# First convolution stage as pairs of 64-row TensorE tiles: an S5 scan gated with an H3 long convolution

## The chip, the cores and the metric

The kernel runs on one core of one Trainium2 chip. The metric is device time in microseconds (us). All kernels of one comparison were run in turns with the kernel before on the same chip. A run is called slow when it lies over 1.5% above the fastest run of the same kernel, otherwise fast; averages and ratios here use fast runs. On one core the times of one kernel spread by up to 18 us, so differences below 1% are not read as differences.

## The reference

`S = 2048`, `D = 1024`, batch 1, bfloat16. `A` is a diagonal complex scan, `B` a long convolution by FFT, and a scalar gate for each row mixes them. Cut to what matters:

```python
def _B_ref(q, k, v, shift_k, ssm_k, ssm_D):          # q is A's x
    k_shift = ...                                    # causal filter of 4 taps per channel
    kv = k_shift * v
    y = irfft(rfft(pad(kv)) * rfft(pad(ssm_k)))[:S]  # causal convolution, length 2 S
    y = y + kv * ssm_D[None, None, :]                # the skip weight: one number per channel
    return q * y

g = sigmoid((x * gate_w).sum(-1, keepdims=True))
return g * _A_ref(...) + (1 - g) * _B_ref(x, ...)
```

## The kernel before

The transform of B is three products on TensorE. The channels come in 8 units of 128; of each unit the filter (K) and the input (V) are transformed. TensorE writes its products to PSUM, where this kernel has four tiles of 1024 columns; an evacuation copies such a tile to SBUF, from which the next step reads. A tile of K or V holds 8 channels x 16 time blocks on its 128 partitions, and `NG = 16` groups of 8 channels along the free dimension. The skip weight of a channel is added to sample 0 of its filter, so the tile `sdz` must hold the 8 channels of each group at partitions 0, 16, 32, ... 112.

```python
sdz = parm.tile([128, D // 8], BF16, name="sdz")
nc.vector.memset(sdz, 0.0)
...
dma("POOL", 0.6, lambda: [sdz[0:128:16, :]], lambda: [B_ssm_D.rearrange("(g c) -> c g", c=8)], [], [e_sdz], -200, issue=1.3)
...
def load_A(src, u, tag, ex, pr):                       # K and V tiles of unit u
    t = pl.tile(tag, [NG, 128], cap=CAPS[tag])
    ...
    dma("SP", 2.6, lambda: [t.ap],
        lambda: [src[u * CH:(u + 1) * CH, :].rearrange("(g c) (n m) -> (c n) g m", c=8, m=128)], ...)
    return t

def load_K(u, pr):
    ka = load_A(B_ssm_k, u, "ka", [], pr)
    op("POOL", 0.25, lambda: G.tensor_tensor(out=ka.ap[:, :, 0], in0=ka.ap[:, :, 0],
                                             in1=sdz[:, u * NG:(u + 1) * NG], op=ALU.add), ...)     # line 712
    return ka

def stage1(a, z, w, hh, q, pr):                        # first stage: half of the frequencies, 8 groups
    ps = pl.psum([8, 128])
    def f():
        for i in range(8):
            PE_.matmul(ps.ap[:, i, :], lhsT=a.ap[:, 8 * q + i, :],
                       rhs=t1v[:, hh * 128:(hh + 1) * 128], start=True, stop=True)                   # line 747
    ...
    evac(...)                                          # 1024 columns of PSUM to SBUF: line 520

def spec(z, kv, q, h, pr):                             # second stage: K and V in one product
    ...                                                # 512 + 256 + 256 columns: lines 760 to 762
...
for hh in range(2):
    z = pl.tile("z", [8, 2, 2, CH], cap=CAPS["z"])
    for w, a in ((0, ka), (1, va)):
        for q in range(2):
            stage1(a, z, w, hh, q, PU[u][4 + hh])
    ...
```

`op`, `dma` and `evac` only record work. A list scheduler in the kernel then puts all of it into one fixed order for each engine, from tables of priorities (`PS`, `PU`, ...) and limits on buffers (`CAPS`). Each engine runs its list in that order.

Of the kernel before, what the change touches and what calls it, by code (L numbers as in the profile page):

```python
# [317 lines left out]
def kernel(  # L318
# [35 lines left out]
    CH = 128  # L354
# [24 lines left out]
    sdz = parm.tile([128, D // 8], BF16, name="sdz")  # L379
# [116 lines left out]
    tab1 = tabB.tile([128, 16, 2, 8], BF16, name="tab1")  # L496
# [22 lines left out]
    def evac(o_, i_, r, w, prio):  # L519
# [14 lines left out]
        [-427.2, -1083.5, 24.9, -780.9, -204.2, -1089.3, -324.2, -515.8, 71.9, -210.3, -1260.0],  # L534
        [-705.1, -403.6, -901.1, -494.7, -729.5, -287.3, 776.9, -570.5, -705.6, -264.3, -450.7],
        [-241.3, -302.5, -542.0, -230.8, 110.9, -574.5, 18.1, 98.8, 142.7, -769.2, -1187.5],
        [-225.3, 90.4, 3.4, -430.0, -212.3, -234.6, 58.5, -724.3, -681.9, -757.6, -1901.0],
        [-528.6, -87.6, -252.8, 51.9, 179.0, -229.1, -57.5, 217.6, 119.4, -179.2, -15.2],
        [221.2, 154.3, -430.1, -56.0, 24.2, 36.2, -482.5, -303.7, 42.6, -546.0, -514.0],
        [-484.3, -185.5, 228.0, -404.7, 149.7, -608.8, -117.9, -305.2, -587.6, -145.3, 214.0],  # L540
        [-81.2, 181.0, -870.6, -304.1, 273.2, -35.7, 66.5, 89.8, 407.7, 271.4, -321.5],
    ]
    PU = [
        [-862.5, -1665.1, -1164.4, -497.9, -793.6, -334.9, -898.2, -892.9, -899.2, 53.0, -342.8, -919.3, -1021.7, -1138.5],
        [-1197.2, -576.0, -1859.3, -750.4, -783.4, 108.2, -1211.7, -134.4, -1391.3, -625.7, -695.6, 142.7, -637.3, -830.0],
        [-883.6, -901.4, -2192.4, -135.2, -397.8, -167.7, -1038.5, -632.4, -741.0, -663.6, -443.3, -348.2, -828.9, -1858.3],
        [-422.2, -1524.9, -3002.1, -1789.7, -1628.2, 76.7, -624.4, -596.7, -1807.9, -986.0, 184.4, -868.7, -1101.3, -453.1],
        [-1177.7, -1058.3, -1227.0, -197.3, -955.1, 51.0, -1415.8, -423.8, -625.9, -1309.6, -1493.1, -858.4, -368.7, -1156.3],
        [160.1, -1665.5, -1080.4, -319.6, -1177.1, 24.7, -1055.3, -275.2, -281.5, -3.8, -843.5, -1118.8, -63.9, -235.7],
        [231.4, -1719.5, -1931.1, -946.9, -964.7, -516.2, -2023.7, -1096.3, -1171.2, -731.8, -165.3, -925.9, -519.7, -974.1],  # L550
        [-2013.4, -1902.6, -1933.6, -1026.0, -1145.7, -1011.7, -2629.3, -759.8, -1134.2, -798.7, -1034.3, -1752.8, -590.0, -664.0],
    ]
    PO = [
        [377.3, 600.4, -823.5],
        [377.4, 168.1, -139.0],
        [-920.1, 1298.4, -120.6],
        [151.9, 1173.6, -754.1],
        [-377.5, 767.6, -407.2],
        [-390.4, 1063.7, -1054.5],
        [-355.6, 9.3, -1223.6],  # L560
        [-280.7, 495.1, -101.3],
        [189.0, 211.4, 204.3],
        [326.3, 111.7, -677.7],
        [-344.9, 809.2, -296.6],
        [-174.6, 1110.7, -1287.9],
        [-133.8, -647.5, -506.5],
        [-72.6, 147.9, 591.6],
        [58.1, 1181.8, -738.2],
        [-520.2, 1310.1, -136.3],
    ]  # L570
    PC = [
        [88.8, 259.5],
        [91.2, 5.4],
        [216.3, -500.6],
        [296.5, 69.5],
        [-522.8, 410.3],
        [-241.8, -85.2],
        [-663.7, 231.4],
        [-168.9, -283.4],
    ]  # L580
    PH = [-489.3, 277.9, -35.3, -417.3, -0.7, -305.5, -324.5, -501.8]
    PG = [-435.2, -508.5, -1259.5, -564.5, -677.8, 588.3]
    PX = [95.0, 1.8]
    CAPS = {"zb": 9, "Hc": 10, "tab": 7, "z": 10, "kv": 6, "qq": 9, "ra": 3, "rb": 12, "kT": 1, "vT": 2, "acc": 1, "ka": 1, "va": 1, "pp": 1,
            "tmpj": 2, "t1": 2, "xn": 3, "xt": 4, "pb": 5, "ot": 10, "BT": 2, "xs": 3, "dg": 7, "cw": 4, "tgZ": 8, "frt": 5, "rqt": 10, "Hk": 12}
    SPARE, NBIG, NKEEP, NPX = 0, 4, 4, 1
# [3 lines left out]
    dma("POOL", 0.6, lambda: [sdz[0:128:16, :]], lambda: [B_ssm_D.rearrange("(g c) -> c g", c=8)], [], [e_sdz], -200, issue=1.3)  # L590
# [27 lines left out]
    def tables0():  # L618
# [12 lines left out]
        v2c, v2s = sl(88, 16), sl(104, 16)  # L631
        v1 = pl.tile("tg4", [16, 2], F32, cap=1)
# [25 lines left out]
        def c():  # L658
            TT(out=tab1.rearrange("p k r c -> p (k r) c"),
               in0=v1.ap.rearrange("p k r -> p (k r)").unsqueeze(2).to_broadcast([128, 32, 8]),  # L660
               in1=mask().unsqueeze(1).to_broadcast([128, 32, 8]), op=ALU.mult)
            for vt, tt in ((v2c, tabFc), (v2s, tabFs)):
                TT(out=tt, in0=vt().unsqueeze(2).to_broadcast([128, 16, 8]),
                   in1=masks().unsqueeze(1).to_broadcast([128, 16, 8]), op=ALU.mult)
# [36 lines left out]
    def conv():  # L701
        def load_A(src, u, tag, ex, pr):
            t = pl.tile(tag, [NG, 128], cap=CAPS[tag])
            ex = ex + ([(xT[0, NC - 1], 1)] if u < 2 else [])
            dma("SP", 2.6, lambda: [t.ap],
                lambda: [src[u * CH:(u + 1) * CH, :].rearrange("(g c) (n m) -> (c n) g m", c=8, m=128)],
                ex, [t], pr, alt="POOL", alt_issue=1.8)
            return t

        def load_K(u, pr):  # L710
            ka = load_A(B_ssm_k, u, "ka", [], pr)
            op("POOL", 0.25, lambda: G.tensor_tensor(out=ka.ap[:, :, 0], in0=ka.ap[:, :, 0], in1=sdz[:, u * NG:(u + 1) * NG], op=ALU.add),  # L712
               r=[ka, e_sdz], w=[ka], prio=pr)
            return ka
# [27 lines left out]
        def stage1(a, z, w, hh, q, pr):  # L742
            ps = pl.psum([8, 128])

            def f():
                for i in range(8):
                    PE_.matmul(ps.ap[:, i, :], lhsT=a.ap[:, 8 * q + i, :], rhs=t1v[:, hh * 128:(hh + 1) * 128],  # L747
                               start=True, stop=True)
            op("PE", 8 * 0.058, f, r=[a, e_t1, (e_g, 0), (e_g, 1)], w=[ps], prio=pr)
            evac(lambda: z.ap[:, :, w, :, 64 * q:64 * q + 64].rearrange("p k r (g c) -> p k r g c", c=8), lambda: ps.ap.rearrange("p g (k r c) -> p k r g c", r=2, c=8),  # L750
               r=[ps], w=[(z, (w, q))], prio=pr)

        def spec(z, kv, q, h, pr):
            ps = pl.psum([2, 2, 2, CH])

            def f():
                for i in range(2):
                    k2 = 4 * q + 2 * h + i
                    zz = z.ap[:, k2 % 8]
                    PE_.matmul(ps.ap[:, i], lhsT=fC[:, k2, :], rhs=zz, start=True, stop=False)  # L760
                    PE_.matmul(ps.ap[:, i, :, 0, :], lhsT=fS[:, k2, :], rhs=zz[:, :, 1, :], start=False, stop=False)  # L761
                    PE_.matmul(ps.ap[:, i, :, 1, :], lhsT=fN[:, k2, :], rhs=zz[:, :, 0, :], start=False, stop=True)  # L762
            op("PE", 2 * (MM(512) + 2 * MM(256)), f, r=[z, e_f], w=[ps], prio=pr)
            evac(lambda: kv.ap[:, :, :, 2 * h:2 * h + 2, :].rearrange("p w r k c -> p k (w r) c"), lambda: ps.ap.rearrange("p k w r c -> p k (w r) c"), r=[ps], w=[(kv, h)], prio=pr)
# [49 lines left out]
        for u in range(NU):  # L814
# [5 lines left out]
            for hh in range(2):  # L820
                z = pl.tile("z", [8, 2, 2, CH], cap=CAPS["z"])
                for w, a in ((0, ka), (1, va)):
                    for q in range(2):
                        stage1(a, z, w, hh, q, PU[u][4 + hh])
                for q in (2 * hh, 2 * hh + 1):
                    pr = PU[u][6 + q]
                    kv = pl.tile("kv", [2, 2, 4, CH], cap=CAPS["kv"])
                    spec(z, kv, q, 0, pr)
                    spec(z, kv, q, 1, pr + 1.0)
                    pp = product(kv, pr + 2.0)  # L830
                    inverse(pp, zb, q, pr + 3.0)
# [4 lines left out]
    def s5():  # L836
# [159 lines left out]
        wps = pl.psum([2, 512])  # L996

        def keep():
            i2 = ident.unsqueeze(1).to_broadcast([128, 2, 128])
            for _ in range(16):  # L1000
                for j in range(2):
                    PE_.matmul(wps.ap[64 * j:64 * j + 64, 0, 0:128], lhsT=ident[:, 64 * j:64 * j + 64], rhs=ident, start=True, stop=True)
            for _ in range(6):
                for j in range(2):
                    PE_.matmul(wps.ap[64 * j:64 * j + 64, 0, 0:256].rearrange("p (a b) -> p a b", b=128), lhsT=ident[:, 64 * j:64 * j + 64],
                               rhs=i2, start=True, stop=True)
            for _ in range(5):
# [183 lines left out]
```

## Time and profile before

| | before |
|---|---|
| time, median (3 runs) | 435.83 us (435.67 to 2371.7; the last figure is one stray run) |
| profiled run | 428.82 us, span 427.0, fast |
| TensorE busy | 398.4 us, 93% of the span |
| VectorE, ScalarE, GpSimd busy | 346.7, 267.8, 132.7 us |

In the page's picture of the span in 40 slices of 10.7 us, each digit is a busy share in tenths; PEclk is the clock that TensorE was granted. From the third slice on TensorE is nearly full, at full clock.

```profile
PE   7598999999999789999969999899989999999996
PEclk9999999999999999999998999999999999999999
```

The costliest groups are given as: engine and operation, count | busy us, mean ns of one | idle before them. Evacuating 1024 columns takes 1.04 us, and a first-stage product of eight matmuls is one such evacuation.

```profile
L520 ACT CAST slab<-ps 128x1024 bf16<-128x1024 f32 x197 | 185.4, 1042 | 62.8 <-PE ps L892 17.6
...
L747 PE MATMUL ps<-tab,slab 128*128 128x128 bf16 x512 | 35.0, 222 | 7.5 <-POOL slab L712 6.2
```

The list of DMA issues gives size of one transfer and median time from issue to landing: the 2 KB of skip weights take longer than the 8 KB of short-filter taps on the same queue.

```profile
skb<-in_B_shift_k_dram POOLq DMA_DIRECT2D x1, 8.0 KB, 6.3
sdz<-in_B_ssm_D_dram POOLq DMA_DIRECT2D x1, 2.0 KB, 10.2
```

### The profile page before, as it was taken

To read this page: it belongs to the slowest core of one execution; us is meant where nothing else is said; L and a number is where in the kernel's file an instruction comes from. 1 tells how busy PE (TensorE), PEld (TensorE's weight loads), DVE (VectorE), ACT (ScalarE), POOL (GpSimd) and SP (SyncE) were. 2 spreads that over 40 slices of the span, in tenths; PEclk is the share of its full clock that TensorE was granted. 3 is DMA by queue.
4 is the path that set the end of the run, shared out by engine and by line. 5 is a ranking of instruction groups with operands and counts; after the bars stand their busy time and mean duration, and the time that the engine had idled before them with its cause. 6 is when DMAs were issued, how large, how long until landed. Compare 5 with 4: busy or idle time off the path is not lost.

```text
span 427.0 us, 7194 instructions
## 1 busy us (share of the span) xinstructions
PE 398.4 (93%) x2691; PEld 228.5 (54%) x2736; DVE 346.7 (81%) x513; ACT 267.8 (63%) x310; POOL 132.7 (31%) x172
## 2 busy tenths in 40 slices
PE   7598999999999789999969999899989999999996
PEld 6353544655566456566635655676544444444442
DVE  4998999999979789989889989979696969724422
ACT  3489488747589679477966786999554286203100
POOL 6994611232464134753634403340010000000000
PEclk9999999999999999999998999999999999999999
DMA  8999999459999999598999369999989996405111
GB/s 149 113 196 195 194 232 231 174 90 160 158 186 193 256 217 185 127 207 173 187 184 164 90 192 166 287 184 178 174 163 185 213 234 205 143 22 177 49 37 62
DMA packets 153596, 71.87 MB, mean 168 GB/s; under 512 B 129861, under 2 KB 147541, under 8 KB 153561
## 3 DMA queue, kind: packets, MB, share of 16 engines
q1 hardware_dynamic: 146120, 54.55, 69.8%
q0 software_dynamic: 7360, 16.85, 16.9%
q8 instruction: 21, 0.34, 0.4%
q14 instruction: 15, 0.11, 0.1%
q10 hardware_dynamic: 80, 0.01, 0.0%
HBM read 24.93 MB, written 16.79 MB: 98 GB/s over the span
## 4 chain that ended last, share of the span: by engine, by line
PE 68%; DMA 11%; SPq 10%; ACT 4%; DVE 3%; issue 3%; POOL 0%; DVEq 0%; ACTq 0%; POOLq 0%
PE ps L1125 22%; PE ps L882 20%; SPq L513 8%; DMA slab<-slab 5%; PE ps L760 4%; ACT slab L520 4%; PE ps L747 4%; DMA slab<-in_A_x_dram 4%; PE ps L889 3%; PE ps L950 3%; DMA slab<-in_B_ssm_k_dram 3%; PE ps L761 2%; PE ps L786 2%; PE ps L762 2%; SPq L515 2%
## 5 line engine op out<-in xcount | busy, mean ns | idle before, releaser
L520 ACT CAST slab<-ps 128x1024 bf16<-128x1024 f32 x197 | 185.4, 1042 | 62.8 <-PE ps L892 17.6
L882 PE MATMUL ps<-slab,slab 128*128 128x512 bf16 (+1 forms) x527 | 115.8, 370 | 6.3 <-DMA slab<-in_A_B_re_dram 3.1
L1125 PE MATMUL ps<-slab,slab 128*128 128x512 bf16 x485 | 109.1, 379 | 1.0 <-DVE slab L1134 0.4
L882 PEld LDWEIGHTS <-slab 128*128 128x128 bf16 x544 | 52.8, 99 | 60.0 <-issue 5.5
L1125 PEld LDWEIGHTS <-slab 128*128 128x128 bf16 x512 | 49.8, 98 | 59.6 <-issue 0.7
L515 POOL DMA_DIRECT2D slab<-slab x84 | 51.4, 618 | 57.8 <-ACT slab L520 51.9
L1134 DVE SCALAR_TENSOR_TENSOR slab<-ps,gcols,slab 128x512 bf16<-128x512 f32 x32 | 23.6, 747 | 39.1 <-PE ps L1125 36.1
L1107 ACT ACTIVATE slab<-slab,omgc 128x512 bf16<-128x512 bf16 x32 | 21.2, 714 | 45.2 <-DMA slab<-pB_scr 40.1
L760 PE MATMUL ps<-slab,fC 128*128 128x512 bf16 x118 | 44.9, 381 | 1.1 <-ACT slab L520 0.6
L747 PE MATMUL ps<-tab,slab 128*128 128x128 bf16 x512 | 35.0, 222 | 7.5 <-POOL slab L712 6.2
L911 DVE TENSOR_TENSOR slab<-slab,slab 128x2048 bf16<-128x2048 bf16 x31 | 37.7, 1217 | 3.5 <-PE ps L747 1.5
L772 DVE TENSOR_TENSOR slab<-slab 128x2048 bf16<-128x2048 bf16 x32 | 38.6, 1215 | 1.8 <-ACT slab L520 1.5
L747 PEld LDWEIGHTS <-slab 128*128 128x128 bf16 x512 | 31.4, 99 | 12.3 <-POOL slab L712 6.8
L761 PE MATMUL ps<-slab,fS 128*128 128x256 bf16 x128 | 35.0, 273 | 0.6 <-issue 0.2
L762 PE MATMUL ps<-slab,fN 128*128 128x256 bf16 x128 | 35.0, 274 | 0.0
L786 PE MATMUL ps<-slab,gC 128*128 128x256 bf16 x128 | 29.9, 273 | 1.7 <-DVE slab L776 1.7
L776 DVE TENSOR_TENSOR slab<-slab 128x512 bf16<-128x512 bf16 x64 | 24.9, 416 | 6.3 <-PE ps L950 2.3
L788 PE MATMUL ps<-slab,gS 128*128 128x128 bf16 x128 | 28.0, 219 | 0.0
L787 PE MATMUL ps<-slab,gN 128*128 128x128 bf16 x128 | 28.0, 219 | 0.0
L735 DVE TENSOR_TENSOR slab<-slab,slab 128x2047 bf16<-128x2047 bf16 (+2 forms) x22 | 26.7, 1213 | 0.0
L808 DVE TENSOR_TENSOR slab<-ps,slab 128x1024 bf16<-128x1024 f32 x16 | 19.3, 1216 | 3.3 <-PE ps L806 2.8
L1113 DVE SCALAR_TENSOR_TENSOR slab<-slab,gcols,slab 128x512 bf16<-128x512 bf16 x26 | 18.3, 745 | 3.5 <-ACT slab L1107 3.4
(184 smaller groups left out, 532.5 us busy)
## 6 DMA issues: line engine op xcount, KB each, us to landing
slab<-in_A_x_dram SPq DMA_DIRECT2D x22, 256.0 KB
slab<-slab POOLq DMA_DIRECT2D x84, 64.0 KB, 5.3
slab<-h_scr SPq DMA_DIRECT2D x8, 512.0 KB
slab<-pB_scr SPq DMA_DIRECT2D x16, 256.0 KB
out_dram<-slab SPq DMA_DIRECT2D x15, 256.0 KB
slab<-in_B_ssm_k_dram SPq DMA_DIRECT2D x7, 512.0 KB
pB_scr<-slab SPq DMA_DIRECT2D x12, 256.0 KB
slab<-slab SPq DMA_DIRECT2D x44, 64.0 KB
```

The source lines that it names most:

```text
L513: nc.sync.dma_start_transpose(out=o_, in_=i_)
L515: QS[q].dma_start(out=o_, in_=i_)
L520: op("ACT", 1.04, lambda: A.copy(o_(), i_()), r=r, w=w, prio=prio, alt=("DVE", 1.2, lambda: V.tensor_copy(o_(), i_())))
L747: PE_.matmul(ps.ap[:, i, :], lhsT=a.ap[:, 8 * q + i, :], rhs=t1v[:, hh * 128:(hh + 1) * 128], start=True, stop=True)
L760: PE_.matmul(ps.ap[:, i], lhsT=fC[:, k2, :], rhs=zz, start=True, stop=False)
L761: PE_.matmul(ps.ap[:, i, :, 0, :], lhsT=fS[:, k2, :], rhs=zz[:, :, 1, :], start=False, stop=False)
L762: PE_.matmul(ps.ap[:, i, :, 1, :], lhsT=fN[:, k2, :], rhs=zz[:, :, 0, :], start=False, stop=True)
L772: TT(out=T.ap, in0=K.unsqueeze(2).to_broadcast([128, 2, 2, 4 * CH]), in1=W_.unsqueeze(1).to_broadcast([128, 2, 2, 4 * CH]), op=ALU.mult)
L786: PE_.matmul(ps.ap[:, i], lhsT=gC[:, k2, :], rhs=pp.ap[:, :, i, :], start=True, stop=False)
L882: PE_.matmul(ps.ap[:, ri, k0:k1], lhsT=BT.ap[:, d, ri, :], rhs=t.ap[:, d, k0:k1], start=(d == 0), stop=(par == 1 and d == ND - 1))
L911: TT(out=out, in0=tab.ap.unsqueeze(2).to_broadcast([128, 2, 2, CW]), in1=x.unsqueeze(1).to_broadcast([128, 2, 2, CW]), op=ALU.mult)
L1125: PE_.matmul(ps.ap, lhsT=Hr[pi, a // 4].ap[:, par, ri, (a % 4) * 128:(a % 4 + 1) * 128], rhs=CT[pi, dh][0].ap[:, CT[pi, dh][1], ri, :], st ...
```

## The change

The first stage multiplies by a block-diagonal table: 8 channels share the 128 rows, so most of the table is zero. The change gives four channels to each half of the rows and runs the halves as two 64-row tiles of TensorE side by side. A table for four channels is half as wide, so all 16 frequencies fit into 128 columns, and a unit needs half the steps. Around it, K and V get separate tiles `z`, each loaded tile comes as two halves of four-channel groups, the skip weights must stand at four partitions of each half, the warm-up is simplified, and the plan is made anew. The core of the diff, with the tables cut:

```diff
-    sdz = parm.tile([128, D // 8], BF16, name="sdz")
+    sdz = parm.tile([128, D // 4], BF16, name="sdz")
...
-    tab1 = tabB.tile([128, 16, 2, 8], BF16, name="tab1")
+    tab1 = tabB.tile([128, 16, 2, 4], BF16, name="tab1")
... (tables PS, PU, PO, PC, PH, PG, PX and CAPS all replaced; SPARE, NBIG = 0, 4 becomes 3, 3)
-    dma("POOL", 0.6, lambda: [sdz[0:128:16, :]], lambda: [B_ssm_D.rearrange("(g c) -> c g", c=8)], [], [e_sdz], -200, issue=1.3)
+    dma("POOL", 0.6, lambda: [sdz[64 * i:64 * i + 64:16, :] for i in range(2)],
+        lambda: [B_ssm_D.rearrange("(g c) -> c g", c=4)] * 2, [], [e_sdz], -200, n=2, issue=0.9)
...  load_A
-            dma("SP", 2.6, lambda: [t.ap],
-                lambda: [src[u * CH:(u + 1) * CH, :].rearrange("(g c) (n m) -> (c n) g m", c=8, m=128)],
+            dma("SP", 2.6, lambda: [t.ap[64 * i:64 * i + 64] for i in range(2)],
+                lambda: [src[u * CH + 64 * i:u * CH + 64 * i + 64, :].rearrange("(g c) (n m) -> (c n) g m", c=4, m=128) for i in range(2)],
...  load_K: one addition on GpSimd becomes two
...  stage1
-                for i in range(8):
-                    PE_.matmul(ps.ap[:, i, :], lhsT=a.ap[:, 8 * q + i, :], rhs=t1v[:, hh * 128:(hh + 1) * 128],
-                               start=True, stop=True)
+                for g in range(4):
+                    for i in range(2):
+                        rows = slice(64 * i, 64 * i + 64)
+                        PE_.matmul(ps.ap[:, 4 * i + g, :], lhsT=a.ap[rows, 4 * q + g, :], rhs=t1v[rows, :], start=True, stop=True)
...  spec: one product over K and V (512 + 256 + 256 columns) becomes one for each (256 + 128 + 128)
-            for hh in range(2):
-                z = pl.tile("z", [8, 2, 2, CH], cap=CAPS["z"])
-                for w, a in ((0, ka), (1, va)):
-                    for q in range(2):
-                        stage1(a, z, w, hh, q, PU[u][4 + hh])
+            for w, a in ((0, ka), (1, va)):
+                zs.append(pl.tile("z", [16, 2, CH], cap=CAPS["z"]))
+                for q in range(4):
+                    stage1(a, zs[w], q, PU[u][4 + w])
```

## The prediction

> **What bounds the kernel now.** I read the page first for busy shares, then the chain that ended last for what sets the end, then the costliest groups, the waits, and short timeline windows for the cost of single matmuls.
>
> ```profile
> span 427.0 us, 7194 instructions
> PE 398.4 (93%) x2691; PEld 228.5 (54%) x2736; DVE 346.7 (81%) x513; ACT 267.8 (63%) x310; POOL 132.7 (31%) x172
> ...
> PE 68%; DMA 11%; SPq 10%; ACT 4%; DVE 3%; issue 3%; POOL 0%; DVEq 0%; ACTq 0%; POOLq 0%
> ```
>
> TensorE is busy 93% of the span and carries 68% of the chain, so its time counts. Busy time overstates a matmul, because their recorded durations overlap. So I take the step from one start to the next. The chain of the last 120 us gives it for 512 columns, and one piece of the same chain gives it for the first conv stage (line 747):
>
> ```profile
> 80.31 0.27 PE ps L760
> ...
> 95.29 0.89 PE ps L747 x16
> ...
> 353.05 10.74 PE ps L1125 x49
> ```
>
> 10.74 / 49 = 0.219 us per 512-column matmul including the ends (the median step, taken from the starts in the trace, is 0.216), and 0.89 / 16 = 0.056 us per 128-column one. The 256-column step is 0.109 us, the difference of the two starts here:
>
> ```profile
> 80.42 0.27 PE L761 MATMUL ps<-slab,fS 128*128 128x256 bf16 x1
> 80.53 0.27 PE L762 MATMUL ps<-slab,fN 128*128 128x256 bf16 x1
> ```
>
> Multiplying each group by its median step, with some slack for short waits, I get 384 us of TensorE work; of the 421 us between its first and its last matmul some 37 to 42 are idle. About 13 of these lie before 36 us, where the transposed loads of x and B set the pace. The largest later idle times are three of 3.6, 1.8 and 2.9 us at 147, 218 and 222 us. After 311 us, only the output product runs (512 x 0.216 = 110.6 us in all).
>
> VectorE is the next engine: in the stretch from 25 to 300 us it is busy 252 of 275 us, as full as TensorE. ScalarE has room.
>
> **What the Trainium skill says.** (1) "TensorE: Matmul & The Clock Gate", Back-to-back issue gap: a warm matmul takes N/2.4 + 2.5 ns. That is 56, 109 and 216 ns at 128, 256 and 512 columns, and the trace agrees. (2) The same page, Part 3 on packing small matmuls: row tiles at different rows run at the same time, starting about 4 ns apart. (3) "TensorEngine Tiling (Array Packing)", Key Properties: changing the tiling mode drains the engine. The kernel before happens to contain a test of both in its warm-up:
>
> ```profile
> 8.44 0.75 PE L1010 MATMUL ps<-ident 64*64 64x128 bf16 x20
> 9.12 0.50 PE L1014 MATMUL ps<-ident 64*128 64x256 bf16 x6
> 9.55 0.62 PE L604 MATMUL ps<-dskd,ones 128*128 128x128 bf16 x8
> ...
> 37.22 1.69 PE L964 MATMUL ps<-slab,gwb 128*32 128x512 bf16 x27
> 38.84 0.39 PE L882 MATMUL ps<-slab,slab 128*128 128x512 bf16 x1
> ```
>
> Line 1014 is three pairs of 64-row tiles. One such matmul lasts 0.269 us, so the last one starts at 9.12 + 0.50 - 0.27 = 9.35: six matmuls of 256 columns start within 0.23 us, two pair-steps of about 0.115. In single file they would need 5 x 0.109 = 0.55. So pairs do run at once. The drain shows too: the last pair has streamed in by 9.35 + 0.11 = 9.46, but line 604 in full mode starts at 9.55, **about 0.09 us lost**. Leaving the 32-column tiles of the gates (lines 964 to 882) costs the same: the last starts at 38.53, has streamed by 38.74, and 38.84 is the next start. (4) The page on tiling, Gotcha 1: different row tiles must write to different PSUM banks. The new code does so (pair member i writes slots 4i to 4i+3, one bank each).
>
> **The change, part by part.**
> First stage: 512 matmuls of 128 rows and 128 columns become 512 of 64 rows and 128 columns, two at a time. Before: 512 x 0.056 = 28.7 us. After: 256 pairs x 0.056 = 14.3. **Saves 14.3 us.** The evacuations stay 64 of 1024 columns; ScalarE's copies last 0.99 to 1.17 us over very different patterns, so runs of 4 instead of 8 elements should not matter.
> Second stage (lines 760 to 762): each product over K and V together (512 + 256 + 256 columns) becomes one for each. 384 matmuls (128 x 0.216 + 256 x 0.109 = 55.6 us) become 768 (256 x 0.109 + 512 x 0.056 = 56.6). **Adds 1.0 us.** The inverse (lines 786 to 788) already has this 256 + 128 + 128 shape and steps by 0.109 + 0.056 + 0.056, so the doubled weight loads stay hidden.
> Mode switches: each unbroken run of first-stage matmuls now costs a drain going in and one going out, some 0.19 to 0.20 us. In the trace of before, line 747 falls into 28 runs of 8 to 56 matmuls, mostly 16. With 28 to 45 runs after, **adds 5.5 to 9 us, say 7**; the plan's own estimate of a stage-one product (four times 0.058) has no term for it. If each of the 64 products stood alone it would be 12.8.
> K load: the buffer of the filter is single, and before its last reader is the second half-pass of the first stage, which comes late. Of unit 3, the K load goes out at 140.2 us, just after the previous unit's last first-stage run at 140.0, and TensorE waits:
>
> ```profile
> PE ps L747 <- POOL slab L712: 6.2, 2, 3.5
> ...
> PE ps L805 <- DMA slab<-slab: 1.6, 1, 1.6
> ```
>
> Line 712 is the addition to the K tile, which waits for that load. After the change all four K products come in one block, whatever V does, so the buffer is freed early. I expect **3 to 5 of these 6.2 us back**.
> Small costs off the path: 16 loads become 32 halves (0.4 to 0.6 us of issue each on SP, some 0.9 on POOL), 8 more POOL additions (about 0.5 us each). POOL is 31% busy. They delay a K tile by about 1 us where it is waited for. The warm-up products lie before 9.6 us, ahead of the wait for x, and change nothing.
> Sum: -14.3 + 1.0 + 7 - 4 + 1 = **-9.3 us** if all of it lies on the path, which TensorE's share of the chain supports. 435.8 - 9.3 = 426.5.
>
> **The rivals.**
> *The mode switches eat it.* If first-stage products are scattered singly, the switch costs 12.8 us and the first stage saves 1.5. For it: PSUM holds four of these 1024-column tiles, and one evacuation takes 1.04 us against 0.22 us for a product, so a run of four can rarely follow another. Against: 28 runs before, not 64. Time then: 431 to 435.
> *VectorE becomes the bound.* It is as full as TensorE from 25 to 300 us and its work does not change; at most some 20 us could come out of this stretch. For it: 91% busy. Against: it has 3% of the chain, and 13 us of its copies and some 22 us of scaling by the short filter's taps can go to ScalarE. Its effect would be half of the gain: 431.
> *The new plan is better or worse by itself.* All priorities and buffer counts change, and about 25 us of TensorE idle after the start depends on them. Fewer 8 KB slabs for the big tiles (three for four) could make one unit wait for the last; or the search could find fewer waits. Either way some 4 us.
> *Full gain:* drains hidden in waits that exist anyway, all K waits gone: 435.8 - 14.3 + 1 - 6 = 416.5, unlikely as TensorE has few waits to hide drains in.
>
> **Range and chances.** The centre is the sum, 426.5 us. Switches may be 2 to 5 us off, the plan 4, the K wait 3; together about 6 us to each side, so 419 to 434. Faster by over 2% means below 427.1, almost at my centre; I give it 0.52, within 2% 0.45. Slower by over 2% (above 444.5) would need a plan with 18 us of new waits: 0.03.
>
> **What the profile after should show.** The first-stage line with 512 matmuls of 64x128, a run of 8 spanning four pair-steps of 0.056 (0.22 us to the last start's end against 0.45 before), and a gap of about 0.1 us at each end of a run. Second-stage groups of 256 and 512 matmuls at steps of 0.109 and 0.056. About 30 to 45 runs. ScalarE and VectorE busy times within 3 us of before. The wait for the line that adds to the K tile below 3 us. I would be wrong if pairs step by more than 0.07 us at 128 columns (the pairs seen in before had 256, which leaves twice the time for two weight loads), if the drain into row tiles is larger than out of them, or if TensorE's idle time grows by more than 5 us.

## More of the kernel before

The timeline of SyncE (start, length, instruction) shows when the transposing loads of x go out. The queue issues the last six in 19.6 us, and the first transpose of k follows at 32.76 us.

```profile
13.16 19.55 SPq L513 DMA_TRANSPOSE slab<-in_A_x_dram  x6
32.76 3.86 SPq L513 DMA_TRANSPOSE slab<-in_B_k_dram  x1
```

## The result

| | before | after |
|---|---|---|
| time, median | 436.0 us (4 runs; one stray at 2371.7) | **470.03 us** (466.13 to 475.18) |
| ratio of fast runs, 95% interval | | **1.069** [1.063, 1.075] |
| same kernels on a second chip | 430.66 (fast mean 428.8) | 458.74 (fast mean 457.6), ratio 1.065 [1.052, 1.077] |

The change makes the kernel slower by 6 to 7%. A ratio is the mean time of one kernel's fast runs over that of the other's of the same rounds, so it is not quite the ratio of the medians. The profile taken with the first result fell into a slow run (472.57 us), so I read the changed kernel from the second chip's profile, a fast run of 460.42 us.

The page of the changed kernel, span, busy times and chain:

```profile
span 458.6 us, 8038 instructions
PE 399.3 (87%) x3069; PEld 235.5 (51%) x3110; DVE 353.5 (77%) x512; ACT 267.4 (58%) x312; POOL 149.4 (33%) x197
...
PE 58%; SPq 14%; DMA 11%; ACT 7%; DVE 6%; issue 2%; POOL 1%; another core or an unknown queue 0%; DVEq 0%; ACTq 0%; POOLq 0%
```

TensorE gives 10 points of the chain away, 4 of them to SyncE's queue and 3 each to ScalarE and VectorE. The 40 slices (11.5 us each here) show where:

```profile
PE   7436696998999799999599989696899999999996
PEclk9856798999999999999979999998999999999999
```

Slices 3 to 5 read 3, 6 and 6 where before they read 9, 8 and 9, and the granted clock falls to 0.5 of full speed in slice 3. In windows of both kernels (stretch, length, busy us of PE, PEld, DVE, ACT and POOL, then granted clock, DMA share and GB/s), first before:

```profile
12.00:34.00 22.00, 16.83 (x93) 9.62 (x95) 21.65 (x40) 14.32 (x17) 21.45 (x12) 0.92 1.25 153
34.00:55.00 21.00, 19.41 (x140) 9.72 (x142) 19.66 (x24) 14.82 (x20) 9.49 (x9) 1.00 1.15 206
```

then after:

```profile
12.00:34.00 22.00, 8.01 (x41) 4.10 (x40) 21.43 (x45) 13.42 (x18) 19.74 (x13) 0.66 1.39 43
34.00:55.00 21.00, 13.17 (x57) 7.01 (x58) 4.18 (x5) 4.64 (x3) 6.09 (x5) 0.66 1.17 159
```

The DMA engines are as busy as before and move 43 GB/s instead of 153. From 12 to 55 us TensorE does 98 matmuls instead of 233. In SyncE's timeline the last six transposes of x take 40.6 us instead of 19.6, and everything behind them in the fixed order comes 20 us later:

```profile
12.12 40.63 SPq L513 DMA_TRANSPOSE slab<-in_A_x_dram  x6
...
52.80 2.87 SPq L513 DMA_TRANSPOSE slab<-in_B_k_dram  x1
```

The list of TensorE's waits (us in total, times, longest) has two waits of over 10 us for these loads, which in the kernel before were 3.1 us (B) and 2.1 us (x):

```profile
PE ps L891 <- DMA slab<-in_A_B_im_dram: 10.7, 1, 10.7
PE ps L891 <- DMA slab<-in_A_x_dram: 10.5, 2, 6.8
PE ps L757 <- ACT slab L520: 7.3, 14, 1.1
...
PE ps L757 <- POOL slab L719: 3.6, 2, 2.7
```

The third line is new as well: the first stage (now line 757) waits for evacuations on ScalarE, 7.3 us against 1.1. The fourth is the wait for the K tile, now 3.6 us instead of 6.2.

**First theory.** What changed at the start, apart from the plan, is the load of the skip weights. It went from one transfer of 1024 two-byte elements on 8 partitions to two transfers of 1024 elements on 4 partitions each, and both are in flight while x is transposed:

```profile
sdz<-in_B_ssm_D_dram POOLq DMA_DIRECT2D x2, 2.0 KB, 21.5
```

The first lands 15.8 us after its issue and the second 27.2 us. Nothing waits for `sdz` so early; it is a bad neighbour, not a dependency. **The rival** is the new plan (other order, other buffer limits), which puts other work at the start. A second question is why the first stage's shorter work does not show.

### The profile page after: what moved, and what is told of

The parts are those of the page before. It is cut to its first block, busy times and chain, and to the rows that moved or that the text cites. A ratio compares the mean times of both kernels' runs of the same rounds, so it can differ in the third digit from the quotient of the medians.

```text
span 470.8 us, 8079 instructions
## 1 busy us (share of the span) xinstructions
PE 407.1 (86%) x3110; PEld 239.1 (51%) x3110; DVE 353.6 (75%) x512; ACT 267.6 (57%) x312; POOL 146.1 (31%) x197
## 4 chain that ended last, share of the span: by engine, by line
PE 55%; DMA 14%; SPq 13%; DVE 7%; ACT 5%; POOL 2%; issue 2%; DVEq 0%; POOLq 0%; ACTq 0%
PE ps L1119 23%; SPq L513 13%; PE ps L891 11%; DMA slab<-in_B_k_dram 6%; ACT slab L520 5%; PE ps L769 4%; DMA slab<-slab 3%; DMA slab<-in_A_x_dram 3%; PE ps L795 2%; PE ps L959 2%; PE ps L771 2%; PE ps L770 2%; DMA pB_scr<-slab 2%; PE ps L757 1%; DVE slab L743 1%
## 5 line engine op out<-in xcount | busy, mean ns | idle before, releaser
L520 ACT CAST slab<-ps 128x1024 bf16<-128x1024 f32 x189 | 178.4, 1037 | 102.8 <-PE ps L891 25.4
L891 PE MATMUL ps<-slab,slab 128*128 128x512 bf16 (+1 forms) x544 | 122.7, 383 | 21.3 <-DMA slab<-in_A_x_dram 13.1
L891 PEld LDWEIGHTS <-slab 128*128 128x128 bf16 x544 | 54.4, 102 | 81.9 <-issue 23.0
L1119 PEld LDWEIGHTS <-slab 128*128 128x128 bf16 x512 | 49.9, 98 | 59.0
L769 PE MATMUL ps<-slab,fC 128*128 128x256 bf16 x256 | 57.6, 272 | 0.0
L1128 DVE SCALAR_TENSOR_TENSOR slab<-ps,gcols,slab 128x512 bf16<-128x512 f32 x32 | 23.7, 747 | 43.8 <-PE ps L1119 43.7
L771 PE MATMUL ps<-slab,fN 128*128 128x128 bf16 x256 | 56.1, 219 | 0.0
L770 PE MATMUL ps<-slab,fS 128*128 128x128 bf16 x256 | 56.0, 219 | 0.0
L520 DVE CAST slab<-ps 128x1024 bf16<-128x1024 f32 x19 | 23.0, 1218 | 15.9 <-PE ps L891 10.2
L757 PE MATMUL ps<-tab,slab 64*128 64x128 bf16 x512 | 23.9, 238 | 12.1 <-ACT slab L520 6.1
L757 PEld LDWEIGHTS <-slab 64*128 64x128 bf16 x512 | 17.8, 104 | 20.7 <-issue 15.6
L771 PEld LDWEIGHTS <-fN 128*128 128x128 bf16 x256 | 25.0, 98 | 2.9
```

The costliest lines, as they stand in the source:

```text
L520: op("ACT", 1.04, lambda: A.copy(o_(), i_()), r=r, w=w, prio=prio, alt=("DVE", 1.2, lambda: V.tensor_copy(o_(), i_())))
L757: PE_.matmul(ps.ap[:, 4 * i + g, :], lhsT=a.ap[rows, 4 * q + g, :], rhs=t1v[rows, :], start=True, stop=True)
L769: PE_.matmul(ps.ap[:, i], lhsT=fC[:, k2, :], rhs=zz, start=True, stop=False)
L770: PE_.matmul(ps.ap[:, i, 0, :], lhsT=fS[:, k2, :], rhs=zz[:, 1, :], start=False, stop=False)
L771: PE_.matmul(ps.ap[:, i, 1, :], lhsT=fN[:, k2, :], rhs=zz[:, 0, :], start=False, stop=True)
L891: PE_.matmul(ps.ap[:, ri, k0:k1], lhsT=BT.ap[:, d, ri, :], rhs=t.ap[:, d, k0:k1], start=(d == 0), stop=(par == 1 and d == ND - 1))
```

## The experiments

"Wrong" marks kernels whose numbers are not the reference's. The comparison on the chip passed these too, so passing it says little here; that a result is right rests on reading its edit.

### 1. The load of after in the kernel before

Order and plan stay as they were; only the tile `sdz` is made twice as wide to take the load. The skip values are wrong, because the four-channel layout does not fit the old tiles.

```diff
-dma("POOL", 0.6, lambda: [sdz[0:128:16, :]], lambda: [B_ssm_D.rearrange("(g c) -> c g", c=8)], ...)
+dma("POOL", 0.6, lambda: [sdz[64 * i:64 * i + 64:16, :] for i in range(2)],
+    lambda: [B_ssm_D.rearrange("(g c) -> c g", c=4)] * 2, ...)
```

> The kernel before, same plan and order, with one thing taken from the change: the skip weights are loaded by its two transfers of 4 partitions x 256 two-byte elements (2048 elements in all) in place of one of 8 x 128 (1024). The skip term comes out wrong on purpose. Theory A (this load holds up the transposed loads of x on the DMA engines until it has drained): x is there some 12 to 18 us later than in before, the first matmul stalls grow by that much, time 448 to 456 us. Theory B (the loss of the change is in its plan and in waits for PSUM, the small load is harmless): 435 to 439 us.

Measured: 445.44 us median, ratio 1.036 [1.021, 1.051]. Its fast runs average 444.7 us, 15.5 us over the kernel before's 429.1 of the same rounds. SyncE's timeline and the list of DMA issues:

```profile
12.58 31.74 SPq L513 DMA_TRANSPOSE slab<-in_A_x_dram  x6
...
sdz<-in_B_ssm_D_dram POOLq DMA_DIRECT2D x2, 2.0 KB, 20.5
```

A transfer that nothing waits for costs 15 us. The six transposes take 31.7 us instead of 19.6, and from 12 to 34 us the core moves 51 GB/s instead of 153. GpSimd's own work does not explain it: its load of x goes out at 36.66 us instead of 35.64. Theory A had expected a little more, 448 us at least.

### 2. The same weights in another form, in both kernels

The weights are loaded as contiguous runs of 16 bytes (two of 8 in the changed kernel) on 128 partitions on ScalarE's queue, spread by a copy, and turned by one matmul with the identity during the warm-up (two in the changed kernel). The result is right.

```diff
+nc.scalar.dma_start(out=sdr, in_=B_ssm_D.rearrange("(g c) -> g c", c=8))
+nc.vector.memset(sdl, 0.0)
+nc.vector.tensor_copy(sdl[:, 0:128:16], sdr)
-dma("POOL", 0.6, lambda: [sdz[0:128:16, :]], ...)
 ... in the warm-up:
+PE_.matmul(wps.ap[:, 0, 0:128], lhsT=sdl, rhs=ident, start=True, stop=True)
+V.tensor_copy(sdz, wps.ap[:, 0, 0:128])
```

> The kernel before, same plan, with the skip weights loaded in one contiguous transfer of 128 rows of 16 bytes and spread over the partitions by one matmul with the identity; result right. Theory A: the transposed loads of x, which in before slow down from 10.7 to 18 us while the two-byte elements trickle, no longer do; 428 to 433 us. Theory B: 435 to 437 us.

> The changed kernel, same plan, with the skip weights loaded contiguously and spread by two matmuls; result right. Theory A: it wins back the 20 us by which its x arrives later than in before, 444 to 452 us, and what is left over 436 is plan and PSUM. Theory B: 460 to 467 us.

Measured: the kernel before 426.15 us, ratio 0.997 [0.985, 1.008]; the changed kernel 437.52 us with two of four runs slow, ratio 1.009 [0.990, 1.028]. Both are below what theory A had expected (428 to 433 and 444 to 452 us). Both were run again in five rounds:

> The kernel before with only the contiguous load of the skip weights, again, now beside the other three of this group. Theory A: 425 to 429 us, 1% under before.

> The changed kernel with contiguous skip weights, split loads kept, on the same chip: 434 to 440 us.

Measured: 429.70 us, ratio 1.002 [0.998, 1.007], and 432.48 us, ratio 1.005 [0.999, 1.011]; the first just over its expected range, the second under it. The repaired changed kernel's timeline:

```profile
11.65 18.67 SPq L519 DMA_TRANSPOSE slab<-in_A_x_dram  x6
30.36 2.27 SPq L519 DMA_TRANSPOSE slab<-in_B_k_dram  x1
```

Its six transposes take 18.7 us instead of 40.6, and its time falls from 457.6 to 430.9 us (means of fast runs on the same chip, in different rounds). **About 25 of the 29 us are this load.** The rest of the change, plan included, leaves the time where it was. In the kernel before the load is free to within 1%. So neither repaired version clearly beats the kernel before. The repair changes the form and the queue at once. The queue alone can hardly be the cause: the short-filter taps, 8 KB in runs of 8 bytes on 128 partitions, stay on GpSimd's queue in every kernel (4.7 us in flight in the repaired one). But the same two-byte form on another queue was not run.

### 3. What in the load costs: elements, or partitions

Two variants of the kernel before separate the two. One keeps 1024 elements, in two transfers on four partitions (values wrong). The other makes the old transfer on eight partitions twice (values right).

```diff
 b_sdz_4p     + [sdz[64*i:64*i+64:16, :] for i in range(2)]  <-  [B_ssm_D.rearrange("(i g c) -> i c g", i=2, c=4)[i] for i in range(2)]
 b_sdz_twice  + [sdz[0:128:16, :], sdz[0:128:16, :]]         <-  [B_ssm_D.rearrange("(g c) -> c g", c=8)] * 2
```

> The kernel before, same plan, its 1024 two-byte skip weights loaded by two transfers over 4 partitions each in place of one over 8 (values wrong on purpose). If the cost goes by the number of elements: as before, 428 to 434 us. If it goes by the number of partitions that share the transfer[...]: 438 to 446 us.

> The kernel before, same plan, its load of the skip weights over 8 partitions done twice, 2048 elements in all (result right). If the cost goes by the number of elements: 440 to 446 us, like the 445.4 us with the load of the change. If it goes by partitions: 430 to 435 us.

> The changed kernel itself once more, on the chip of this group, to compare with the two next to it. Theory: within 2% of its 467 to 470 us; before 425 to 436 us.

Measured: 437.67 us, ratio 1.020 [1.011, 1.030], and 436.46 us, ratio 1.018 [1.009, 1.027]. Neither lies in a range given for it; the first is just under the one for partitions. The changed kernel itself, run beside them, gave the 458.74 us of the result. Their lines in the list of DMA issues, 4 partitions first:

```profile
sdz<-in_B_ssm_D_dram POOLq DMA_DIRECT2D x2, 1.0 KB, 10.7
```

```profile
sdz<-in_B_ssm_D_dram POOLq DMA_DIRECT2D x2, 2.0 KB, 10.0
```

The two variants cost 2.0% and 1.8%, and the full form 3.6%. That looks like two causes that add up, but the runs do not separate elements from partitions as I had meant them to: both variants also make two transfers of one. And in the second, GpSimd issues the second transfer only when the first has landed, as its timeline shows:

```profile
8.43 1.13 POOL L515 DMA_DIRECT2D sdz<-in_B_ssm_D_dram  x1
17.27 1.07 POOL L515 DMA_DIRECT2D sdz<-in_B_ssm_D_dram  x1 [7.72 <-DMA sdz<-in_B_ssm_D_dram]
```

All of GpSimd's work behind it is late, its load of x at 41.09 us instead of 35.64, so part of the 1.8% can be this wait. Two transfers of 512 elements over all eight partitions would be the missing test; it was not run. What can be said is that the packet counts of GpSimd's DMA queue move with the time. Taking the load out of the kernel before (experiment 2) removes 48 packets, so the load was 48; the two variants come to 96 each, and the full form to 160. In time that is 0, about 8, about 8 and 15 us on top of the kernel before, whose own 48 packets cost nothing measurable.

The six transposes take 23.6 and 23.7 us in the variants. In each of the three forms the kernel loses 3 to 5 us more than the transposes grow. The clock granted to TensorE from 12 to 34 us falls too, from 0.92 to 0.84 in the variants and 0.66 with the full form; whether that is the rest was not tested.

The Trainium skill bears on both halves of this. "DMA: Bandwidth & Descriptors", Rules for kernel authors, says that a strided last dimension "lowers to one descriptor per element" and should be rearranged to be contiguous, and that the slowest dimension of a transfer sets how many of the 16 DMA engines share it. The runs agree with the first in direction: the contiguous form removes the cost. On the second they are silent, as above. The trace records packets, not descriptors, so the count per element itself is not seen.

That the same load costs 15 us in the old plan and about 25 in the new is not explained by an experiment. I could not exchange the plans: the tables of one kernel with the code of the other end in a plan that cannot be completed, in both directions. The traces narrow it, though. The six transposes grow by 12 us in the old plan and by 22 in the new (40.6 us, from 18.7 once repaired), so the difference arises there. The first two of the six take 20.9 us in experiment 1 and 25.0 in the changed kernel, the last four 10.8 and 15.6. Beside those last four, GpSimd sends out the loads of a K tile and of x (in experiment 1 only that of x, at 36.66 us):

```profile
37.62 1.73 POOL L515 DMA_DIRECT2D slab<-in_B_ssm_k_dram  x2
39.34 0.91 POOL L515 DMA_DIRECT2D slab<-in_A_x_dram  x1
```

In the repaired kernel they go out at almost the same time, but there the last transpose of x has ended at 30.3 us. So a queue that was held up once runs into transfers that it would otherwise have been ahead of. This is read from the traces; no run tests it.

### 4. The pairs alone

The kernel before, with only the first stage's eight matmuls turned into four pairs of 64-row tiles. The table is the old one, so the values are wrong. Plan and order are unchanged, and each pair is one 64-row piece of each of two groups, so the TensorE time of the stage halves as in the change.

```diff
-for i in range(8):
-    PE_.matmul(ps.ap[:, i, :], lhsT=a.ap[:, 8 * q + i, :], rhs=t1v[:, hh * 128:(hh + 1) * 128], ...)
+for g in range(4):
+    for i in range(2):
+        rows = slice(64 * i, 64 * i + 64)
+        PE_.matmul(ps.ap[:, 4 * i + g, :], lhsT=a.ap[rows, 8 * q + 4 * i + g, :], rhs=t1v[rows, hh * 128:(hh + 1) * 128], ...)
```

> The kernel before, same plan and order, with only its first-stage products run as pairs of 64-row tiles (each group uses half of its rows, so the result is wrong on purpose; operands, shapes of outputs and evacuations are unchanged). The prediction's sum: 14.3 us less streaming, some 28 runs x 0.19 us of drains, so 9 us less TensorE work, and as TensorE is on the path 426 to 429 us. Rival (a product of 0.22 us against an evacuation of 1.04 us only moves the wait to PSUM): 433 to 437 us.

Measured: 433.42 us, ratio 1.002 [0.986, 1.019]; two of the four runs count as slow. The 9 us less that the prediction's sum asks for, 2%, lie outside the interval: the halved stage brings nothing that can be seen. Its trace is of a slow run, so it is a hint only: line 749, the first stage, waits 10.3 us for the K tile (6.2 before) and 6.3 us for evacuations (1.1 before).

### 5. Full rows in the repaired changed kernel

The counter-test: everything of the repaired change, but the products of the first stage over 128 rows, one at a time (wrong). If pairs are worth their 14.3 us less 3.4 for mode switches, this must be some 11 us slower.

```diff
-PE_.matmul(ps.ap[:, 4 * i + g, :], lhsT=a.ap[rows, 4 * q + g, :], rhs=t1v[rows, :], start=True, stop=True)
+PE_.matmul(ps.ap[:, 4 * i + g, :], lhsT=a.ap[:, 4 * q + g, :], rhs=t1v, start=True, stop=True)
```

> The changed kernel with the contiguous load of the skip weights, and its first-stage products run over all 128 rows again, one after the other (wrong on purpose, as each then sums the channels of both halves); plan, order and evacuations unchanged. TensorE streams 14.3 us more and drains 18 x 0.19 = 3.4 us less. Theory C (the time of the pairs is handed to waits for PSUM, which frees one tile in 1.04 us however short the product): within 3 us of the 437.5 us of the same kernel with pairs. Prediction's step (TensorE is on the path, so its time is the kernel's): some 11 us more, 447 to 450 us.

Measured: 437.63 us median with two slow runs, the fast ones 433.36 and 429.5, ratio 1.007 [0.994, 1.020]. With pairs it was 1.009 and 1.005. Another 11 us, 2.5%, would put it at 1.030 or more, outside the interval: the pairs bring nothing that can be seen here either. First the wait for evacuations with full rows, then with pairs:

```profile
PE ps L762 <- ACT slab L526: 2.1, 8, 0.3
```

```profile
PE ps L762 <- ACT slab L526: 7.3, 16, 0.9
```

I split TensorE's time in the first stage by the starts of its matmuls, over 18 runs of products (both traces fast): "in" goes from the start of the matmul before a run to the run's first, "within" to its last, "out" to the start of the one after it. So "in" and "out" hold one matmul's step each, besides waits and drains:

| us | in | within | out | sum |
|---|---|---|---|---|
| full rows | 3.5 | 33.7 | 4.1 | 41.3 |
| pairs | 5.2 | 26.5 | 9.5 | **41.2** |

The runs are 7.2 us shorter, not 14.3, as they hold more waits inside; and what lies around them is 7.1 us longer. How that looks, in a timeline of the changed kernel's TensorE (start, length, instruction, idle before it and what ended it):

```profile
101.91 0.84 PE L757 MATMUL ps<-tab,slab 64*128 64x128 bf16 x24
103.07 0.40 PE L757 MATMUL ps<-tab,slab 64*128 64x128 bf16 x8 [0.32 <-ACT slab L520]
103.99 0.40 PE L757 MATMUL ps<-tab,slab 64*128 64x128 bf16 x8 [0.52 <-ACT slab L520]
```

Three products go out in 0.84 us. Then the four PSUM tiles are in use, and a product starts only as an evacuation ends, some 1 us after the last. The Trainium skill says so in one line that I had not weighed: "TensorEngine Tiling (Array Packing)", PSUM Bottleneck: "Tiling speeds up TensorE but not PSUM evacuation". The trace agrees.

### 6. More work on either side

If TensorE and the evacuations are in balance, adding to either must cost time. One kernel does each full-row product of experiment 5 twice (28.7 us more for TensorE). The other, with pairs, copies half of each first-stage evacuation a second time (by its trace 0.59 us on ScalarE for 56 of them and 0.69 on VectorE for 8, 38 us in all; result right). These ran on a third chip (kernel before there: 432.38 us), with a kernel for the split loads, below.

```diff
 a_full2_pe
-for g in range(4):
+for g in (0, 1, 2, 3, 0, 1, 2, 3):
 a_ev15_pe
+copy(o_(), i_())
+copy(o_(slice(0, 1)), i_(slice(0, 1)))
```

> The changed kernel with contiguous skip weights, its first-stage products over all 128 rows and each done twice (wrong on purpose): 28.7 us more TensorE streaming than with them once, 43 us more than as pairs; plan, order and evacuations as there. Theory C (a first-stage product of 0.22 to 0.45 us hides behind an evacuation of 1.04 us): still within 8 us of 437.5 us. Prediction's step (TensorE's time is the kernel's): 462 to 468 us.

> The changed kernel with contiguous skip weights and pairs, but each of its 64 first-stage evacuations copies half of its columns a second time (result right): 0.5 us longer each, 35 us more ScalarE time in all, TensorE work the same. Theory C (the evacuations set the pace of the first stage): 450 to 465 us. Prediction's step (TensorE sets it, ScalarE has room at 57 to 63% busy): 437 to 444 us.

Measured: 457.31 us for the doubled products, with three of four runs slow and the fast one 448.54, so no interval; that is 15 to 19 us over the fast runs of experiment 5, on another chip. It fits neither expectation: the doubled products do not hide behind the evacuations, and they do not cost their full time. The longer evacuations: 454.96 us, ratio 1.052 [1.041, 1.063], about 20 us over the repaired kernel's 1.005, as theory C expected. So more of either costs about half of what is added or a little more, and less TensorE work gives nothing. In the first stage the evacuations are as much a bound as TensorE is; the TensorE side of this rests on one fast run. Taking half of the evacuation away would be the direct test. It leaves data unwritten that later work reads, so it was not run.

### 7. The split loads

The repaired kernel before with its loads of K and V split in two halves of 64 partitions (result right), and the repaired changed kernel with one load of 128 partitions (the old eight-channel layout, the evacuation putting the channels in order; result right).

```diff
 b_halves
-[t.ap] <- [src[...].rearrange("(g c) (n m) -> (c n) g m", c=8, m=128)]
+[t.ap[64*i:64*i+64] for i in range(2)] <- [src[...].rearrange("(g h c) (n m) -> h (c n) g m", h=2, c=4, m=128)[i] for i in range(2)]
 a_c8_pe: the reverse; evac to "p k r (g i c)" in place of "p k r (i g c)"
```

> The kernel before with contiguous skip weights, its loads of the filter and of kv split into two transfers of 64 partitions as in the change (result right), plan and order unchanged. If the split loads are part of what is left between the changed kernel (437.5) and before (426 with the same skip load): 430 to 435 us. If they are harmless, as predicted: 425 to 429 us.

> The same with the loads of filter and kv split into two transfers of 64 partitions, on the same chip this time. Theory D (the split loads delay the first stage's operands and all that is queued behind them on the two issuing queues): 8 us or more over the run without the split. Rival (the 443.5 us seen on another chip were that chip's): within 3 us of it.

> The changed kernel's pairs, all 16 frequencies in one product and its plan, but with the channel layout of before: one load of 128 partitions per tile, one addition of the skip weights, contiguous skip weights; half i of the rows holds channels 4i to 4i+3 of each group of eight, and the evacuation puts them back in order (result right). Theory D: the split is what is left, so 426 to 431 us. Rival (the new plan is what is left): 434 to 440 us.

Measured: 443.54 us with three slow runs, the fast one 434.13. In five rounds the medians of the split loads in the old plan and of one load there are 440.80 and 429.70 us, but four of the six split runs are slow. The fast ones give the ratio 1.012 [1.005, 1.018] against 1.002 [0.998, 1.007]: 4 to 5 us, with intervals that touch, and neither of the ranges expected (8 us or more, within 3 us). Why this kernel falls into slow runs so often is not shown. In the new plan one load in place of two gave 434.65 against 432.48 us, ratios 1.009 and 1.005: no difference, and not the gain of theory D. So the split may cost about 1% in a plan made for one transfer, and nothing that can be seen in a plan made for two. It does not explain the result.

## Why the prediction was wrong

**The step that failed outright is the list of "Small costs off the path".** It names the 16 loads that become 32 and the 8 more additions, and leaves out the line in the diff that doubles `sdz` and splits its load. Its cost in the new plan is about 25 of the 29 us on the second chip (experiment 2), and 15 us in the old plan (experiment 1). The rivals have no such term either; the one closest, a worse plan, was given 4 us, and 18 us of new waits a chance of 0.03. Both facts needed were in views I had before me. My text says that before 36 us "the transposed loads of x and B set the pace", and the list of DMA issues shows 2 KB taking 10.2 us on the neighbouring queue. I did not connect them, because nothing waits for `sdz` at that time.

**The step "if all of it lies on the path, which TensorE's share of the chain supports" failed too.** It carried the whole -14.3 us. The pairs save TensorE's time, and none of the program's: full rows and pairs both stand 41 us in the first stage (experiment 5), and pairs alone in the old plan give 1.002 (experiment 4). I had the reason in my own first rival, four PSUM tiles and 1.04 us of evacuation against 0.22 us of product. There I used it to count the mode switches only, not to ask what the stage waits for once its products are short. A share of 68% of the chain says what bounds the kernel now; it does not say that the engine can be made shorter by 14 us before the next one takes over.

**VectorE as the bound**, the second rival, had the right form with the wrong engine. The wait that grew is the one for ScalarE's evacuations.

Point by point, the prices of single operations held, and the counts and what they lead to mostly did not:

| step of the prediction | predicted | the runs |
|---|---|---|
| pair step at 128 columns | 0.056 us | mostly 0.055 to 0.056; members mostly 3 to 6 ns apart, a quarter 17 to 20 |
| drain at each mode change | about 0.09 us | 0.095 in, 0.092 to 0.093 out |
| runs of first-stage products | 28 to 45 | 18, so 18 x 0.19 = 3.4 us, not 7 |
| second stage | 56.6 us | 256 x 0.109 + 512 x 0.056 = 56.6, at measured steps of 109, 56 and 56 ns |
| wait for the K tile | below 3 us (from 6.2) | 3.6 no; 1.6 once repaired |
| ScalarE and VectorE busy within 3 us | 267.8 and 346.7 | 267.4 yes; 353.5 no (+6.8) |
| TensorE idle would grow by less than 5 us | 37 to 42 | 88.1, from 41.8, by the starts: the named sign of being wrong |

The sum was also optimistic in what it took as independent. Corrected for the count of runs it would have been -12.9 us, while the repaired kernel shows +0.5% with an interval from -0.2% to +1.1%. What the new plan itself adds or takes within that cannot be told, because the plans could not be exchanged. That the repaired kernel's 432.48 us lies inside the forecast of 419 to 434 us is luck: the kernel before stood at 432.44 us in the same rounds, so on that chip no gain at all lies inside the range as well.

## What to carry to other kernels

Read every changed line of a diff as a cost, the small loads first: a load of 4 KB that nothing waits for cost 15 to 25 us, made as it was of two-byte pieces on few partitions, in two transfers beside the transposes that set the pace of the start. Which of these properties does it is not separated. Load such a vector contiguously and let TensorE turn it. Before counting a shorter product as a gain, put it beside the evacuation of the same tile: where a product of 0.22 us feeds a copy of 1.04 us and four PSUM tiles lie between, shorter products become waits.

## What the Trainium skill lacked or had wrong

- "DMA: Bandwidth & Descriptors", Rules for kernel authors: it says that a DMA transpose next to ordinary DMAs "needs nothing". That is about correct data; the section does not say what the neighbour does to the time. Here two transfers of 2 KB in two-byte elements beside the transposes of x, with nothing else of weight changed (experiment 1), lowered the core's DMA rate from 153 to 51 GB/s over 22 us and stretched six transposes from 19.6 to 31.7 us.
- The same section has no figure for the cost of one descriptor per element. One transfer of 1024 elements on eight partitions was in flight for 10.2 us and cost nothing measurable; two of 512 on four cost 2.0% of the kernel's time, two of 1024 on four 3.6%.
- The same section says of two transfers to disjoint halves of the partitions not to bother, as they share the same engines, and has no figure. By fast runs the split stood at 1.012 of the kernel before against 1.002 in a plan made for one load, and at 1.005 against 1.009 in a plan made for two: no gain, and no clear cost.
- "TensorEngine Tiling (Array Packing)", Key Properties: the drain at a change of mode has no number. It was 95 ns going into 64-row tiles and 92 to 93 ns coming out.
- "TensorE: Matmul & The Clock Gate", Back-to-back issue gap: it gives sustained steps of about 81 ns at 128 columns and 131 ns at 512. No run here shows them: the steps were 56 and 216 ns, those of the page's formula for a single matmul, and pairs of 64-row tiles kept 56 ns with twice the weight loads.
